# Dilated local attention plus shifted MLP on one core: 64-key attention blocks with the band mask written by TensorE, two heads per key block, source order on every engine

## The chip, the core and the metric

The kernel runs on one core of a Trainium2 chip. The metric is the device time in microseconds. Three runs of the kernel before took 226.71, 226.94 and 227.81 us; their median, 226.94 us, is the time before.

## The reference, cut to what matters

```python
x = A_x                                    # [1, 2048, 512], bf16
xn = layernorm(x)
# A: 32 heads of width 16; query s sees keys s, s-2, ..., s-14 (8 keys, dilation 2)
q, k, v = heads(xn @ wqkv)
logits = where(key >= 0, q.k * 0.25, -1e9)
s = (softmax(logits) . v) @ wo
# B: layer norm again, an MLP with four shifted column groups, a second MLP
h  = gelu(layernorm(xn) @ w1)              # 512 -> 512
hs = concat(shift(h, +1, -1, +2, -2 rows, a quarter of the columns each)) @ w2
x1 = xn + hs
h2 = gelu(layernorm(x1) @ w3) @ w4         # 512 -> 1376 -> 512
return x + s * silu(x1 + h2)
```

Because the dilation is 2, even and odd rows never attend to each other. Both kernels split the 2048 rows into two parities `p` of 1024 rows, and inside a parity the 8 keys are 8 neighbours.

## The kernel before, in words

**First half.** The 2048 rows are four chunks of 512 (two per parity). For each chunk `stage_ln` takes the layer-norm statistics (VectorE) and the power for the reciprocal root (GpSimd). `stage_a1` transposes the normalised rows on TensorE (L289) and copies them to `xnT` (L291); it also makes the row factor of the second layer norm, as four small matmuls (`rrep_ps`, L298) that spread it over the partitions. `stage_a2` multiplies by `wqk` (L317, 32 matmuls of 512 columns per chunk) and by `w1` (L329, 16 matmuls). `stage_b` multiplies by `w2` (L357) and sends the second normalised rows through DRAM to be transposed by a DMA. `stage_w3` multiplies by `w3` (L392, 44 matmuls per chunk). ScalarE takes all of these out of PSUM.

**The mask.** `kT` and `qT` exist twice per parity (e = 0, 1). In copy e the 16 rows of every second head are replaced by 16 rows of a mask factor, so that a 32-row product of keys and queries gives score plus band mask of one head. The factors are built on GpSimd (`build_mask`), written to DRAM, and `fill_mask` spreads them by 16 DMAs of 128 KB per parity and side on the SyncE queue (L224).

**Attention loop.** Nine units per parity: up to 120 queries with 128 keys. Per unit, `scores` runs 2 x 16 matmuls (L461, 32 rows, four row tiles at once) into PSUM tiles s and t, and ScalarE takes four exponentials per unit (L468, 128x960). `values` makes the V rows (L440, 4 matmuls). `weighted` multiplies the exponentials with V and a column of ones (L489, 32 matmuls, four column tiles at once) into tile o, which VectorE copies to `orw` (L496). Between these the loop lays out `w4_tile` (L413, 11 matmuls per 128 rows, one PSUM bank `w`; then VectorE L420, ScalarE tanh L422, VectorE L423) and `final_tile` (L573, 4 matmuls with `wo`; VectorE L582; addition L584).

**Softmax sums.** Three units make a run. `normalise` writes the sums to DRAM (L511), reads them back on 128 partitions (L517) and moves the outputs to `oT` by 8 GpSimd DMAs (L521). `normalise_mid` inverts (L533), writes (L534) and reads the inverses spread out (L539). `normalise_end` multiplies (L545).

**Order.** A scheduler places most instructions. In the loop the instructions wrapped in `pin` keep their source order. The loop's work is laid out by hand in the lists `fill[n]`, and the SyncE queue issues DMAs strictly one after another.

Of the kernel before, what the change touches and what calls it, by code (L numbers as in the profile page):

```python
# [11 lines left out]
F32 = mybir.dt.float32  # L12


@with_exitstack
def kernel(
# [12 lines left out]


    nc = tc.nc
    P = 128
# [15 lines left out]
    NQ = 120  # L48
    PEN = 512.0


    units = [(0, P, 0, P)]
    while units[-1][0] + units[-1][1] < M:
        q0 = units[-1][0] + units[-1][1]
        nq = min(NQ, M - q0)
        units.append((q0, nq, q0 - W, nq + W))
    NU = len(units)


    runs = []  # L60
    for cuts in ((0, 3, 6, NU), (0, 3, 6, NU)):
        runs.append(
            [(a, b, units[a][0], sum(units[u][1] for u in range(a, b))) for a, b in zip(cuts[:-1], cuts[1:])]
        )
    RW = max(r[3] for rs in runs for r in rs)
# [6 lines left out]
    big = ctx.enter_context(tc.tile_pool(name="big", bufs=12))  # L72
    mid = ctx.enter_context(tc.tile_pool(name="mid", bufs=6))
    orwp = ctx.enter_context(tc.tile_pool(name="orwp", bufs=2))
    sm4 = ctx.enter_context(tc.tile_pool(name="sm4", bufs=5))
    fin = ctx.enter_context(tc.tile_pool(name="fin", bufs=3))
    dram = ctx.enter_context(tc.tile_pool(name="dram", bufs=1, space=bass.MemoryType.DRAM))

    mask_d = dram.tile([2, 16, M], BF16, name="mask_d")
    x1n_dram = dram.tile([S, D], BF16, name="x1n_dram")  # L80

# [6 lines left out]
    cnt = {"v": 0, "a": 0, "b": 0}  # L88
# [3 lines left out]
    def layout(**tags):  # L92
        if "stack" in banks:
            banks["stack"].close()
        banks["stack"] = ctx.enter_context(ExitStack())
        for tag, n in tags.items():
            pool = banks["stack"].enter_context(tc.tile_pool(name=f"ps_{tag}", bufs=1, space=bass.MemoryType.PSUM))
            banks[tag] = (pool, n)

    def pst(tag, name):  # L100
        pool, n = banks[tag]
        return pool.tile([P, n, CH], F32, name=name, tag=tag)

    def psa(name):

        cnt["a"] += 1
        return pst("xyz"[cnt["a"] % 3], name)

    def psb(name):
        cnt["b"] += 1  # L110
        return pst("wb"[cnt["b"] % 2], name)[:, 0, :]

    layout(x=2, y=2, z=2, w=1, b=1)

    def pin(ins):
        return tc.keep_in_program_order(ins)
# [4 lines left out]
    for c in range(NCH):  # L121
        p, k = c // 2, c % 2
        n = 1 if c == 0 else 2
        for t0 in range(k * TPC, (k + 1) * TPC, n):
            nc.sync.dma_start(
                out=xn[p][:, t0 : t0 + n, :],
                in_=xv[p, t0 * P : (t0 + n) * P, :].rearrange("(i q) d -> q i d", q=P),
            )
        if c == 0:
            wqk_sb = midt([P, ND, 2 * D], "wqk_sb")  # L130
            nc.sync.dma_start(out=wqk_sb[:, :, 0:D], in_=wqkv_v[:, :, 0:D])
            nc.sync.dma_start(out=wqk_sb[:, :, D : 2 * D], in_=wqkv_v[:, :, D : 2 * D])
            w1_sb = sm4.tile([P, ND, D], BF16, name="w1_sb", tag="s4")
            nc.sync.dma_start(out=w1_sb, in_=B_w1.rearrange("(dt q) n -> q dt n", q=P))
    w2_sb = sm4.tile([P, ND, D], BF16, name="w2_sb", tag="s4")
    nc.sync.dma_start(out=w2_sb, in_=B_w2.rearrange("(g q) n -> q g n", q=P))
    w3_sb = midt([P, ND, F], "w3_sb")
    nc.sync.dma_start(out=w3_sb, in_=B_w3.rearrange("(dt q) f -> q dt f", q=P))
    wv_sb = const.tile([P, ND, D], BF16, name="wv_sb")
    nc.sync.dma_start(out=wv_sb, in_=wqkv_v[:, :, 2 * D : 3 * D])  # L140
    w4_sb = midt([P, NF, D], "w4_sb")
    nc.sync.dma_start(
        out=w4_sb[:, 0 : NF - 1, :],
        in_=B_w4[0 : (NF - 1) * P, :].rearrange("(ft q) n -> q ft n", q=P),
    )
    nc.sync.dma_start(out=w4_sb[0:FL, NF - 1, :], in_=B_w4[(NF - 1) * P : F, :])
    nc.scalar.preload_act_table_set("gelu_apprx_tanh_and_others")


    ident = const.tile([P, P], BF16, name="ident")  # L150
    make_identity(nc, ident[:])
    ones_bf = const.tile([P, P], BF16, name="ones_bf")
    nc.vector.memset(ones_bf[:], 1.0)
    nhalf = const.tile([P, TPC], F32, name="nhalf")
    nc.vector.memset(nhalf[:], -0.5)

    wm = psa("warm_ps")
    for i in range(16):
        nc.tensor.matmul(
            wm[:, i % 2, :], lhsT=ones_bf[:], rhs=ones_bf.unsqueeze(1).to_broadcast([P, TPC, P]),  # L160
            start=True, stop=True,
        )

    def build_mask():  # L170
        gp = nc.gpsimd
        tab = sm4.tile([P, 3, P + 24], BF16, name="m_tab", tag="s4")

        for i, o, v in ((0, 0, -7), (0, 15, 8), (1, 1, -7), (1, 16, 7)):
            gp.iota(
                tab[:, i, o : o + 135].rearrange("p (k t) -> p k t", t=15)[:, ::2],
                pattern=[[0, 5], [1 if o < 15 else -1, 15]], base=v, channel_multiplier=0,
                allow_small_or_imprecise_dtypes=True,
            )
        gp.memset(tab[:, 1, 0:1], -8.0)  # L180
        gp.iota(
            tab[:, 2, 0:P].rearrange("p (g k) -> p g k", k=2), pattern=[[0, P // 2], [-2, 2]], base=1,
            channel_multiplier=0, allow_small_or_imprecise_dtypes=True,
        )

        nc.vector.tensor_tensor(
            out=tab[:, :, 0:P], in0=tab[:, :, 0:P], in1=ident.unsqueeze(1).to_broadcast([P, 3, P]), op=ALU.mult
        )
        g = small.tile([P, 4], F32, name="mg", tag="mg", bufs=1)
        nc.vector.tensor_reduce(out=g[:, 0:3], in_=tab[:, :, 0:P], axis=mybir.AxisListType.X, op=ALU.add)  # L190
        sg, q = g[:, 2:3], g[:, 3:4]
        one = ones_bf[:, 0:W]
        rows = []
        for w in range(2):
            m = small.tile([P, 16, W], BF16, name=f"m_rows{w}", tag=f"mr{w}", bufs=1)
            rows.append(m)
            c, d = g[:, w : w + 1], m[:, 3:11, :]
            gp.memset(m, 0.0)
            gp.memset(d, PEN if w == 0 else 0.0)
            gp.affine_select(  # L200
                out=d, in_=d, pattern=[[1, W], [-1, W]], compare_op=ALU.is_ge if w == 0 else ALU.not_equal,
                fill=-PEN if w == 0 else 1.0, base=0, channel_multiplier=0,
            )
            gp.tensor_scalar(out=d, in0=d, scalar1=sg, scalar2=None, op0=ALU.mult)
            gp.tensor_scalar(out=q, in0=c, scalar1=-1.0 if w == 0 else 1.0, scalar2=c, op0=ALU.add, op1=ALU.mult)
            if w == 0:
                gp.tensor_scalar(out=q, in0=q, scalar1=1.0, scalar2=-PEN, op0=ALU.add, op1=ALU.mult)
                gp.tensor_scalar(out=m[:, 0, :], in0=one, scalar1=q, scalar2=None, op0=ALU.mult)
                gp.tensor_scalar(out=m[:, 1, :], in0=one, scalar1=c, scalar2=2 * PEN, op0=ALU.mult, op1=ALU.mult)
                gp.memset(m[:, 2, :], -PEN)  # L210
            else:
                gp.memset(m[:, 0, :], 1.0)
                gp.tensor_scalar(out=m[:, 1, :], in0=one, scalar1=c, scalar2=None, op0=ALU.mult)
                gp.tensor_scalar(out=m[:, 2, :], in0=one, scalar1=q, scalar2=None, op0=ALU.mult)
        for w in range(2):
            nc.sync.dma_start(out=mask_d[w].rearrange("r (g l) -> g r l", l=W), in_=rows[w])

    def fill_mask(p, w):
        t = (kT[p], qT[p])[w]
        for e in range(2):  # L220
            for gr in range(4):
                r = 32 * gr + DH * (1 - e)
                pin(
                    nc.sync.dma_start(  # L224
                        out=t[e][r : r + DH, :, :], in_=mask_d[w].unsqueeze(1).to_broadcast([DH, ND, M])
                    )
                )


    NV = 2  # L230
    v_aug = []
    for i in range(NV):
        va = const.tile([P, H, 2 * DH], BF16, name=f"v_aug{i}")
        nc.vector.memset(va[:, :, DH : 2 * DH], 2.0)
        v_aug.append(va)

    xnT = [bigt([P, ND, M], f"xnT{p}") for p in range(2)]
    kT = [[bigt([P, ND, M], f"kT{p}{e}") for e in range(2)] for p in range(2)]
    qT = [[bigt([P, ND, M], f"qT{p}{e}") for e in range(2)] for p in range(2)]
    hT = [midt([P, ND, M + 2], f"hT{p}") for p in range(2)]  # L240
    for p in range(2):
        nc.vector.memset(hT[p][:, :, 0:1], 0.0)
        nc.vector.memset(hT[p][:, :, M + 1 : M + 2], 0.0)

    def rsqrt_eps(dst, var):
# [155 lines left out]
    def w4_tile(c, jj, tail=False):  # L401
# [25 lines left out]
        return half  # L427


    oT = {}  # L430
    orw = {}

    def values(p, u):
# [283 lines left out]
```

## Time and profile before

| | |
|---|---|
| median of three runs | 226.94 us (226.71 to 227.81) |
| span of the profiled execution (first to last instruction) | 222.8 us |
| what lies around the span (median less span; the page has no other total) | 4.1 us |
| TensorE busy | 205.6 us (92%) |
| VectorE, ScalarE, GpSimd busy | 130.1, 136.2, 61.9 us |
| first matmul with `wqk` | starts at 10.06 us |
| last `w3` matmul ends, first `values` starts | 109.03 us |
| last `weighted` ends | 199.2 us |

The busy time of TensorE counts matmuls whose modelled ends overlap those of the next ones. What a matmul really costs is the distance from its start to the next start, and idle time is read from the starts.

### The profile page before, as it was taken

The numbers are of one execution on the slowest core, as the hardware profiler recorded it, in microseconds if no ns is written. First come the engines' busy times: TensorE is split into PE (matmuls) and PEld (weight loads), VectorE is DVE, ScalarE is ACT, GpSimd is POOL, SyncE is SP. The second block draws the span as 40 slices with busy tenths as digits, with TensorE's granted clock in tenths as the row PEclk, the third lists the DMA queues.
The fourth block names the chain that finished last, engine by engine and source line by source line (L and its number), as shares of the span: only waits on it lengthen the run. The fifth ranks groups of instructions, "written<-read, shape, count | busy, mean of one in ns | idle before, by whom it ended". The sixth has DMA issues, their size and how long they took to land.

```text
span 222.8 us, 4851 instructions
## 1 busy us (share of the span) xinstructions
PE 205.6 (92%) x1992; PEld 95.3 (43%) x1992; DVE 130.1 (58%) x244; ACT 136.2 (61%) x158; POOL 61.9 (28%) x119
## 2 busy tenths in 40 slices
PE   8799999999999999999869999999969999999961
PEld 2335545444444444444323444444434445454420
DVE  6689964127279683000103566678457857795984
ACT  2086696956913615665457888898776978842110
POOL 1723563502002202000000007015074482947040
PEclk9999999999999999999988999999999999999998
DMA  5999100130390675799995005526650342625222
GB/s 160 371 392 388 47 0 4 4 8 0 122 161 3 171 195 154 170 118 121 119 122 60 0 3 119 157 68 159 209 125 13 101 83 70 154 51 148 67 85 94
DMA packets 32957, 25.60 MB, mean 115 GB/s; under 512 B 16152, under 2 KB 28792, under 8 KB 32936
## 3 DMA queue, kind: packets, MB, share of 16 engines
q1 hardware_dynamic: 30312, 22.16, 42.7%
q0 software_dynamic: 1536, 2.10, 4.9%
q10 hardware_dynamic: 1088, 1.05, 1.3%
q8 instruction: 15, 0.25, 0.5%
q14 instruction: 6, 0.05, 0.1%
HBM read 16.58 MB, written 4.52 MB: 95 GB/s over the span
## 4 chain that ended last, share of the span: by engine, by line
PE 67%; DMA 10%; DVE 8%; ACT 7%; POOL 2%; SPq 2%; issue 2%; DVEq 0%; ACTq 0%
PE w_ps L413 17%; PE qk_ps L317 9%; PE w_ps L392 9%; ACT prob L468 6%; PE w_ps L329 6%; PE w_ps L357 6%; PE s_ps L461 5%; PE v_ps L440 5%; PE wo_ps L573 4%; DMA qT_159<-mask_d 4%; DMA kT_155<-mask_d 4%; PE o_ps L489 3%; DVE l1s L253 2%; SPq L224 2%; DMA oT_1494<-orw 2%
## 5 line engine op out<-in xcount | busy, mean ns | idle before, releaser
L468 ACT ACTIVATE prob<-s_ps 128x960 bf16<-128x960 f32 (+2 forms) x72 | 62.7, 925 | 15.1 <-PE s_ps L461 14.1
L413 PE MATMUL w_ps<-w_sb,h3T 128*128 128x512 bf16 (+1 forms) x176 | 44.9, 390 | 0.0
L392 PE MATMUL w_ps<-x1nT,w_sb 128*128 128x512 bf16 (+1 forms) x176 | 38.3, 379 | 0.0
L397 ACT ACTIVATE h3T<-w_ps 128x1024 bf16<-128x1024 f32 x20 | 20.5, 1024 | 25.6 <-PE w_ps L392 23.3
L521 POOL DMA_DIRECT2D oT_1494<-orw x24 | 12.4, 523 | 68.2 <-DVE orw L496 68.2
L392 PEld LDWEIGHTS <-w_sb 128*128 128x128 bf16 (+1 forms) x176 | 17.6, 100 | 20.4
L413 PEld LDWEIGHTS <-h3T 128*128 128x128 bf16 (+1 forms) x176 | 15.1, 99 | 17.3 <-issue 1.0
L496 DVE CAST orw<-o_ps 128x960 bf16<-128x960 f32 (+2 forms) x18 | 19.7, 1098 | 1.3 <-PE o_ps L489 1.1
L445 DVE CAST v_aug_148<-v_ps 128x512 bf16<-128x512 f32 (+1 forms) x9 | 6.1, 682 | 23.0 <-PE v_ps L440 23.0
L317 PEld LDWEIGHTS <-wqk_sb 128*128 128x128 bf16 x128 | 12.1, 98 | 12.9
L317 PE MATMUL qk_ps<-xnT_152,wqk_sb 128*128 128x512 bf16 x64 | 15.3, 379 | 0.8 <-DVE xnT_152 L291 0.8
L420 DVE TENSOR_TENSOR xn_95<-w_ps,xn_95 128x512 bf16<-128x512 f32 x8 | 5.5, 684 | 16.5 <-PE w_ps L413 16.5
L329 PE MATMUL w_ps<-xn2T,w_sb 128*128 128x512 bf16 x64 | 14.6, 379 | 0.0
L317 PE MATMUL qk_ps<-xnT_153,wqk_sb 128*128 128x512 bf16 x64 | 14.5, 379 | 0.0
L584 POOL TENSOR_TENSOR xo_1715<-sg,xo_1715 128x512 bf16<-128x512 bf16 x8 | 10.4, 1297 | 14.5 <-DVE sg L582 13.4
L362 DVE TENSOR_TENSOR xn_95<-w_ps,xn_95 128x1024 bf16<-128x1024 f32 x4 | 4.9, 1215 | 14.4 <-PE w_ps L357 14.4
L422 ACT ACTIVATE sig<-xn_96 128x512 bf16<-128x512 bf16 x8 | 5.0, 630 | 12.6 <-DVE xn_96 L420 12.6
L521 POOL DMA_DIRECT2D oT_2418<-orw x24 | 12.1, 513 | 1.6 <-DVE orw L496 1.6
L246 POOL TENSOR_SCALAR l3r<-l3m 128x4 f32<-128x4 f32 x4 | 0.9, 232 | 36.7 <-DVE l3m L254 36.7
L440 PE MATMUL v_ps<-wv_sb,xnT_153 128*128 128x512 bf16 (+1 forms) x36 | 9.3, 380 | 2.0 <-DVE sg L582 2.0
L461 PE MATMUL s_ps<-qT_159,kT_155 32*128 32x120 bf16 (+2 forms) x144 | 7.7, 214 | 3.1 <-DMA qT_159<-mask_d 3.1
L573 PE MATMUL wo_ps<-wo_sb,oT_2418 128*128 128x512 bf16 x32 | 7.6, 379 | 2.2 <-DVE oT_2418 L545 2.2
(132 smaller groups left out, 329.3 us busy)
## 6 DMA issues: line engine op xcount, KB each, us to landing
w_sb<-in_B_w_dram SPq DMA_DIRECT2D x1, 1376.0 KB, 9.5
w_sb<-in_B_w_dram SPq DMA_DIRECT2D x1, 1280.0 KB
wqk_sb<-in_A_wqkv_dram SPq DMA_DIRECT2D x2, 512.0 KB
w_sb<-in_B_w_dram SPq DMA_DIRECT2D x2, 512.0 KB, 6.0
xn_96<-in_A_x_dram SPq DMA_DIRECT2D x4, 256.0 KB, 6.9
xo_1715<-in_A_x_dram SPq DMA_DIRECT2D x4, 256.0 KB, 5.5
xo_2325<-in_A_x_dram SPq DMA_DIRECT2D x4, 256.0 KB, 4.5
out_dram<-xo_1715 SPq DMA_DIRECT2D x4, 256.0 KB, 3.8
```

The lines of the kernel that those rows point to most:

```text
L317: nc.tensor.matmul(pt[:, b, :], lhsT=wqk_sb[:, dt, nt * P : (nt + 1) * P], rhs=xnT[p][:, dt, cs], start=(dt == 0), stop=(dt == ND - 1),)
L329: nc.tensor.matmul(pt[:, b, :], lhsT=w1_sb[:, dt, g * P : (g + 1) * P], rhs=xn2T[:, dt, :], start=(dt == 0), stop=(dt == ND - 1),)
L357: nc.tensor.matmul(pt[:, j, :], lhsT=w2_src(p, g, m0), rhs=w2_sb[:, g, :], start=(g == 0), stop=(g == ND - 1),)
L392: nc.tensor.matmul(pt[:fs, ft % 2, :], lhsT=w3_sb[:, dt, ft * P : ft * P + fs], rhs=x1nT[:, dt, :], start=(dt == 0), stop=(dt == ND - 1),)
L397: last["gelu"] = nc.scalar.activation(h3T[:, 2 * a : 2 * a + 2, :], pt, AF.Gelu_apprx_tanh)
L413: nc.tensor.matmul(pt, lhsT=h3[c][:fs, ft, jj * P : (jj + 1) * P], rhs=w4_sb[:fs, ft, :], start=(ft == 0), stop=(ft == NF - 1),)
L440: nc.tensor.matmul(vp[:nk, :], lhsT=xnT[p][:, dt, k0 : k0 + nk], rhs=wv_sb[:, dt, :], start=(dt == 0), stop=(dt == ND - 1),)
L461: nc.tensor.matmul(st[:nk, b, i * nq : (i + 1) * nq], lhsT=kT[p][e][r : r + 32, dt, k0 : k0 + nk], rhs=qT[p][e][r : r + 32, dt, q0 : q0 + ...
L468: nc.scalar.activation(prv[:nk, 2 * h : 2 * h + 2], st[:nk, :, 0 : 4 * nq], AF.Exp, scale=SCALE)
L496: nc.vector.tensor_copy(out=orw[p][:, :, :, q0 - ra : q0 - ra + nq], in_=op[:, :, 0 : 4 * nq].rearrange("p j (s q) -> p j s q", q=nq),)
L521: nc.gpsimd.dma_start(out=oT[p][DH * hh : DH * (hh + 1), :, ra : ra + rw], in_=orw[p][32 * cg : 32 * cg + DH, jj],)
L573: nc.tensor.matmul(pt[:, j, :], lhsT=oT[p][:, dt, (i + j) * P : (i + j + 1) * P], rhs=wo["sb"][:, dt, :], start=(dt == 0), stop=(dt == ND ...
```

## The change

Every engine call goes through a wrapper that keeps it in program order, so the written order is the order on each engine. The other parts:

- **First chunks in halves.** Chunks 0 and 1 are normalised, transposed and multiplied by `wqk` in halves of 256 rows (`columns`, `qk(c, h)`). Warm-up matmuls go from 16 to 11. The row factor goes through DRAM by two DMAs (`row_factor`), not through matmuls.
- **Two heads per key block.** `kT` is one copy. `qT` holds each head pair twice, with the other head's 16 rows multiplied by zero (`sel`), so 32 rows of keys serve two heads.
- **Mask by TensorE.** `build_mask` makes two small tiles `mk`, `mq` on GpSimd; in `scores` 8 matmuls of 512 columns write the mask into PSUM and the 32 score matmuls add to it.
- **64-key blocks.** 17 units: the first 64 rows of both parities together, then 8 per parity of 120 queries, as two blocks of 64 keys by 64 queries that overlap; the overlap is added on VectorE. Per unit there is one exponential of 128x2048, and `weighted` has 64 matmuls of 64 columns.
- **Sums.** Ten runs (1, 2 x 7, 1, 1 units), inverted two units and applied three units after the last of the run.
- **V copies** go from VectorE to ScalarE.

The diff, cut to its core:

```diff
+class InOrder:
+    def __getattr__(self, name):
+        f = getattr(self.engine, name)
+        def call(*args, **kwargs):
+            return self.tc.keep_in_program_order(f(*args, **kwargs))
+        return call
...
-    NQ = 120
+    KB = P // 2
+    QU = P - W
+    NU = (M - KB) // QU
+    units = [KB - W + u * QU for u in range(NU)]
+    order = [(None, 0)] + [(p, u) for p in range(2) for u in range(NU)]
+    NN = len(order)
+    runs = [(0, 0)] + [(a, a + 1) for a in range(1, NN - 2, 2)] + [(NN - 2, NN - 2), (NN - 1, NN - 1)]
...
-    for i in range(16):
+    for i in range(11):
...
+    def row_factor(c):
...
+        pool.tensor_tensor(out=rb, in0=r2, in1=nhalf, op=ALU.pow)
+        sp.dma_start(out=row_dram[c].rearrange("(j q) -> q j", q=P), in_=rb)
+        rr = fin.tile([P, CH], BF16, name="rrow", tag="f")
+        sp.dma_start(out=rr, in_=row_dram[c].unsqueeze(0).to_broadcast([P, CH]))
...
+    def columns(c, h, evict):
...
+        if evict == "both":
+            act.activation(dst[:, :, 0:P], pt[:, :, 0, :], AF.Copy)
+            dve.tensor_copy(out=dst[:, :, P:], in_=pt[:, :, 1, :])
...
+    def qk(c, h=None, between=()):
...
+                    act.activation(qT[p][:, n0 : n0 + per, e, ms], pt, AF.Identity, scale=sel[:, e : e + 1])
...
+    stats(0, 0)
+    stats(0, 1)
+    rstd(0, 0, 2)
+    stats(0, 2)
+    norm(0, 0)
+    norm(0, 1)
+    columns(0, 0, "both")
+    stats(0, 3)
+    rstd(0, 2, 4)
+    stats(1, 0)
+    norm(0, 2)
+    norm(0, 3)
+    qk(0, 0, {6: [lambda: columns(0, 1, "dve")]})
...
+    layout(s=4, o=2, w=1, b=1)
...
+    def scores(n):
...
+        for s in range(2):
+            off = 0 if p is None or s else W
+            for r in range(4):
+                rows = slice(2 * DH * r, 2 * DH * r + 2 * DH)
+                pe.matmul(
+                    t[KB * s : KB * s + KB, r, :], lhsT=mk[rows, :],
+                    rhs=mq[rows, off : off + KB].unsqueeze(1).to_broadcast([2 * DH, 2 * ND, KB]),
+                    start=True, stop=False, tile_position=(2 * DH * r, KB * s),
+                )
+        for dt in range(ND):
+            for s in range(2):
...
+                for r in range(4):
+                    rows = slice(2 * DH * r, 2 * DH * r + 2 * DH)
+                    pe.matmul(
+                        t[KB * s : KB * s + KB, r, 2 * KB * dt : 2 * KB * (dt + 1)].rearrange("p (e q) -> p e q", e=2),
+                        lhsT=kT[pp][rows, dt, k0 : k0 + KB], rhs=qT[pp][rows, dt, :, q0 : q0 + KB],
+                        start=False, stop=(dt == ND - 1), tile_position=(2 * DH * r, KB * s),
+                    )
...
+        act.activation(pr, st.pop(n).rearrange("p r (i q) -> p r i q", q=KB), AF.Exp, scale=SCALE)
...
+    def weighted(n):
...
+            for s in range(2):
+                for cg in range(4):
+                    h = 4 * jj + cg
+                    pe.matmul(
+                        op[32 * cg : 32 * cg + 32, s, g * KB : (g + 1) * KB],
+                        lhsT=va[KB * s : KB * s + KB, dt * 8 + h, :],
+                        rhs=pr[KB * s : KB * s + KB, h // 2, 2 * dt + h % 2, :],
+                        start=True, stop=True, tile_position=(KB * s, 32 * cg),
+                    )
...
+            dve.tensor_copy(out=wide(ow, c, KB, m), in_=wide(ov_, 0, CH + W, m))
+            mix = small.tile([P, 2 * ND, W], F32, name="mix", tag="mix")
+            dve.tensor_copy(out=mix, in_=ov_[:, 1, :, 0:W])
+            dve.tensor_tensor(out=ow[:, :, c + m : c + KB], in0=ov_[:, 0, :, m:KB], in1=mix, op=ALU.add)
+        if n == b:
+            sums_out(i)
...
+    w4_at = {n: n for n in range(14)}
+    final_at = {n: divmod(n - 6, 8) for n in range(6, 17)}
+    values(0)
+    for n in range(NN):
+        scores(n)
+        gate_tanh()
+        exps(n)
+        gate_mult()
+        t = w4_at.get(n)
+        if t is not None:
+            w4_part(t, 0, 3)
+        if n in final_at:
+            final(*final_at[n])
+        if t is not None:
+            w4_part(t, 3, 6)
+        if n > 0:
+            weighted(n - 1)
+        for i, (a, b) in enumerate(runs):
+            if b == n - 3:
+                sums_apply(i)
+            if b == n - 2:
+                sums_invert(i)
+        if t is not None:
+            w4_part(t, 6, NF)
+        if n + 1 < NN:
+            values(n + 1)
...
+    weighted(NN - 1)
+    layout(f=1, g=1, h=1, i=1, o=2, w=1, b=1)
+    R = len(runs)
+    w4_part(14, 0, NF)
+    final(1, 3, "f", dve)
+    store(nc.sync, 1, 2)
+    sums_apply(R - 3)
+    sums_invert(R - 2)
+    gate_tanh()
+    gate_mult()
+    w4_part(15, 0, NF, "b")
+    sums_invert(R - 1)
+    final(1, 4, "g")
+    final(1, 5, "h")
+    gate_tanh()
+    gate_mult()
+    store(nc.sync, 1, 4)
+    sums_apply(R - 2)
+    final(1, 6, "i", dve)
+    sums_apply(R - 1)
+    final(1, 7, "f", dve)
+    store(nc.scalar, 1, 6)
```

`sums_out`, `sums_invert` and `sums_apply` hold the same steps as `normalise`, `normalise_mid` and `normalise_end`; the last run's DMAs go through ScalarE's queue. `w4_part` is `w4_tile` with the gate's tanh and multiplication moved to the start of the next unit (`gate_tanh`, `gate_mult`); `final` is `final_tile`.

## The prediction, made before the changed kernel was run

> **What bounds the kernel now.** First the page: engine totals and the chain that ended last.
>
> ```profile
> PE 205.6 (92%) x1992; PEld 95.3 (43%) x1992; DVE 130.1 (58%) x244; ACT 136.2 (61%) x158; POOL 61.9 (28%) x119
> ...
> PE 67%; DMA 10%; DVE 8%; ACT 7%; POOL 2%; SPq 2%; issue 2%; DVEq 0%; ACTq 0%
> ```
>
> TensorE bounds most of the span, but a third of the chain lies elsewhere. Then the timeline, TensorE alone, for real costs (start to next start). Sixteen `w1` matmuls at 31.84 in the chain take 3.45 us: 0.2156 us per 512-column matmul. All dense ones are 744, so 160.4 us. Transposes take 0.81/12 = 0.067 us. Sixteen score matmuls take 0.34 us; 32 of `weighted` 0.53.
>
> ```profile
> 160.55 0.39 PE L489 MATMUL o_ps<-prob,v_aug_148 64*32 64x56 bf16 x32
> 160.87 1.04 PE L440 MATMUL v_ps<-wv_sb,xnT_153 128*128 128x512 bf16 x4
> ```
>
> At 56 columns 32 of them take 0.32 us. The two sizes (56 and 120 columns) fit 0.13 us per group plus a quarter of the columns at 0.42 ns each (0.2156/512): four tiles run at once, 5.9 ns per instruction at 56 columns.
>
> Then the stages by time. Work from the first `wqk` matmul (10.06) to the last `w3` (109.03) is 432 x 0.2156 = 93.1 plus 64 transposes and row-factor matmuls at 0.067 = 4.3; only 1.6 us are idle. From 109.03 to 222.8 (113.8 us) the work is 312 x 0.2156 = 67.3 plus 18 units x (0.68 + 0.53) = 21.8, so 89; 25 us are idle. Where:
>
> ```profile
> 109.99 0.23 PE L461 MATMUL s_ps<-qT_158,kT_154 32*128 32x128 bf16 x2
> ...
> 112.29 1.28 ACT L468 ACT_TABLE_LOAD   x1 [2.42 <-PE s_ps L461]
> ...
> 114.08 0.21 PE L461 MATMUL s_ps<-qT_159,kT_155 32*128 32x128 bf16 x1 [0.98 <-DMA qT_159<-mask_d]
> ```
>
> The first scores wait 4.0 us (4.35 less 0.34 of work) for the mask DMAs of `fill_mask`. By the windows the clock is then halved:
>
> ```profile
> 112.00:114.00 2.00, 0.43 (x8) 0.14 (x6) 0.00 (x0) 1.70 (x2) 0.00 (x0) 1.00 1.06 119
> 114.00:116.00 2.00, 1.92 (x11) 0.85 (x11) 0.00 (x0) 1.52 (x2) 0.00 (x0) 0.79 1.11 123
> 116.00:118.00 2.00, 2.00 (x20) 0.67 (x18) 0.00 (x0) 0.00 (x0) 0.00 (x0) 0.50 1.06 119
> ```
>
> The third last column is the granted clock. About 3.4 us at half speed cost 1.7 us more. From 153.7 to 168.2 (14.5 us) the matmuls need 10.3; the largest part is VectorE waiting for `oT`, and TensorE behind it:
>
> ```profile
> 142.86 0.73 DVE L533 RECIPROCAL rb<-dn 128x92 bf16<-128x92 bf16 x1 [1.83 <-DMA dn<-den_d_1495]
> ...
> 165.71 0.91 DVE L545 TENSOR_TENSOR oT_1494<-oT_1494,orw 128x1440 bf16<-128x1440 bf16 x1 [2.37 <-DMA oT_1494<-orw]
> 166.53 0.68 DVE L582 TENSOR_TENSOR sg<-wo_ps,xn_95 128x512 bf16<-128x512 f32 x1
> ```
>
> Up to 198 four exponentials per unit (1.83 us a pair, 62.7 us in all) hold TensorE in most units. After 199.2 the tail is 23.6 us for 76 matmuls (16.4).
>
> **Start, in halves.** VectorE gets a third `v_aug` fill (0.48) before the statistics, which so start at 3.2, not 2.90. Each tile's statistics now end before the next begins (0.66 + 0.16 + 0.03): two tiles end at 4.9. GpSimd adds 0.23 + 1.05 (L246, L247): 6.3. Normalising at 0.36 each: 7.0. The eight transposes end at 7.45, ScalarE and VectorE copy one after the other: first `wqk` matmul 8.2 against 10.06. `wqk` is there: by the page's DMA row 1.9 MB have landed by then, and the x chunk and `wqk` are 1.5. Matmuls of 256 columns stream in 0.107, still above the 0.067 that a transpose shows with its weight load, so halves cost nothing. From 8.2: 93.1 + 56 transposes x 0.067 (3.8) + waits. I put the waits at 1.9: 0.6 for chunk 2's normalisation, 0.5 for `scaled_columns(3)` behind the mask building on GpSimd and two DMAs, 0.8 for VectorE finishing statistics before the second `w2` additions. Bounds 0.4 and 4. End of `w3`: **107.0** (before 109.03). The 11 warm-up matmuls at 0.43 end at 5.75. In this trace the warm-ups change pace at 5.9, so the clock may still be half afterwards: 0 to 1.7 us more (the 3.4 us above); I take 0, the pauses after it being about 1 us.
>
> **One unit on TensorE.** Scores: 8 matmuls of 512 columns and 32 of 128. With four tiles at once (as every row here) 2048 columns, 0.85 + 0.13 = 0.98 us; with eight (four row tiles by two column halves) 0.43 + 0.13 = 0.56. Before: 0.68. No row shows both tilings at once. Each alone reaches its full number of tiles here, so I take 0.56. `weighted`: 64 of 64 columns, 0.34 (eight at once) to 0.56 (four); at the 5.9 ns row 0.38 + 0.13 = 0.51, which I take. V stays 0.86. A unit is 2.37 (`w4`) + 0.56 + 0.51 + 0.86 = 4.31, with `final` (0.86) 5.17.
>
> The Trainium skill speaks against these pieces: TensorEngine Tiling (Array Packing), section Instruction Overhead, gives each matmul about 60 cycles and says not to tile from a dimension that is already small. At 0.42 ns per cycle, 104 matmuls would take 2.6 us per unit, and the sum below would be some 26 us longer. The 56-column row (10 ns each, group cost included) contradicts that.
>
> **One unit on ScalarE and VectorE.** The exponential of 2048 columns, by the slope of 1024 (1.024) and 448 columns (0.528), 0.86 ns each: 1.9 us. With tanh 0.63 and the V copy about 0.6 ScalarE needs 3.1 us a unit; covered by 4.31. VectorE becomes the bound of the loop. After `weighted` it must do: copy of 896 columns 1.08 (slope of L496: 1.21 at 1024, 0.61 at 448), 0.13 and 0.20 for the overlap, then reciprocal or multiplication 0.5, then the `w4` addition 0.61, with 0.2 of handovers: 2.72. Only then may the next `w4` matmul start, as bank `w` is single. Before `weighted` stand 0.65 + 0.86 + 0.65 + 0.51. Period: **5.39** with `final`, 4.53 without. The reciprocal has the `w4` addition queued behind it, and TensorE behind that.
>
> **DMA chain.** From sums written to sums readable on SyncE: 2.0 to 3.9 (median 2.6; six L511 to L517 pairs), then 1.8; inverses 1.6 undisturbed (up to 4.1), then 2.3 (up to 5.2). So the reciprocal comes 4.4 us after the copy and the multiplication 3.9 after the reciprocal. The new order gives 4.53 and 4.0: just in time. I take no wait, but 1.2 for the first run, whose 16 GpSimd DMAs take 16 x 0.51 + 2.3 = 10.5 us against two periods. GpSimd's 4.1 us of issue per run and two additions of 1.3 fit in two periods. The 32 mask DMAs leave SyncE; nothing waits for them any more.
>
> **Tail.** From unit 14 on there is no `w4` in the units, so the DMA chains show. In order: `sums_apply` of run 6 at 8.5 holds `final(16)`; last copy at 14.5; run 7's inverses queue on SyncE behind run 8's sums and land at 19.0; on ScalarE's queue the last gate's tanh stands behind the last run's DMAs, 24.5; last multiplication 27.9; last addition 30.0; store and end 3.3 (219.6 to 222.8 here). **33.3** us from unit 14.
>
> **Sum.** 107.0 + first V 0.86 + unit 0 3.8 (table load and exponential 3.3 beside 3.2) + unit 1 4.3 + 4 x 4.53 + 1.2 + 8 x 5.39 + 33.3 = **211.7** against 222.8: 2.0 gained ahead of the loop, 9.1 behind it. With the 4.1 that the median lies over the span: **215.8 us**.
>
> **Rivals.**
> - *VectorE is not the bound* and the tail is a clean chain: periods 4.31 and 5.17, tail 31, no waits in the first half (105.5): 105.5 + 4.7 + 5 x 4.31 + 8 x 5.17 + 31 = 204, so 208 us. For: 58% busy. Against: the single bank `w`.
> - *Only four tiles at once*: scores 0.98, so TensorE's 5.64 and 4.78 replace the periods: 8 x 0.25 + 4 x 0.25 + 0.8 + 1 in the tail, about 5 more: 221.
> - *Slower: VectorE waits for DMAs in every run.* Place: reciprocal and multiplication, ahead of the `w4` addition. Price: the reciprocal's wait of 1.83 and the multiplication's 0.61 (both seen at 142.9 and 151.2), for each of the seven two-unit runs, 17 us: 233. It decides from 1.6 us per run on (11.1/7). For: before, a run had about one unit more at each step and still waited three times. Against: undisturbed SyncE pairs, no mask DMAs.
> - *Source order does not hold*: the program's listing shows it holding on all engines; no chance given.
>
> A change of 0.5% (1.1 us) is about what can be told from none.
>
> **Chances.** Forecast 0.45, VectorE not the bound 0.2, four tiles 0.18, slower 0.17. A third of the last would stay near 226 or under, and a few of the four-tile cases reach it: faster 0.80, same 0.05, slower 0.15. Range 207 to 228: the low end is the first rival less 1, the high end the slower rival at seven tenths of its price (12 us), which also takes in the half clock at the start and the upper bound of the first half's waits.
>
> **What would show it.** First `wqk` matmul near 8.2, `w3` ending at 107; starts of `values` to `values` 4.5 then 5.4 apart; idle of TensorE ahead of `w4` put down to VectorE; score groups under 0.6 us; the reciprocal and `oT` rows without DMA waits; 33 us from unit 14. I am wrong if the periods exceed 6, if the reciprocal shows a DMA wait in most runs, or if score groups take near 1 us.

## The result, and the profile after

The changed kernel takes **292.4 us** (median of 4 runs, 288.2 to 296.0), the kernel before 226.8 in the runs beside it: 1.283 times as long, interval 1.270 to 1.296. The ratio and its interval, here and below, compare only the faster executions of each kernel. The forecast was 215.8 with a range up to 228. The profiled execution took 290.93 us with a span of 289.1. The page's engine totals and chain, as they were read for the kernel before:

```profile
PE 206.2 (71%) x2612; PEld 104.7 (36%) x2651; DVE 123.4 (43%) x244; ACT 108.5 (38%) x109; POOL 85.1 (29%) x169
...
PEclk9797596599579669999999999899999999975965
...
PE 41%; DMA 31%; DVE 14%; POOL 8%; issue 3%; ACT 0%; SPq 0%; DVEq 0%; POOLq 0%; ACTq 0%
```

TensorE is as busy as before (206 us), but in a span 66 us longer: the work has not grown, waits have come in. A third of the chain is DMA, and the clock row falls to 0.5 again and again in the first two fifths. The chain in order of time names the DMA, and the waits of VectorE and of the SyncE queue sum it up:

```profile
12.41 13.28 DMA row_dram<-r2b
26.61 20.98 DMA row_dram<-r2b
47.60 5.73 DMA rrow<-row_dram
53.35 1.22 DVE xn2T L25
...
73.10 19.33 DMA row_dram<-r2b
92.44 6.22 DMA rrow<-row_dram
```
```profile
DVE xn2T L25 <- DMA rrow<-row_dram: 58.6, 4, 16.6
```
```profile
SPq L25 <- DMA row_dram<-r2b: 75.0, 4, 23.0
```

`row_dram<-r2b` is the row factor's write to DRAM: 1 KB, as 512 packets of 2 bytes. It takes 13 to 23 us four times over; the read that spreads it takes 4 to 6 more. VectorE stands 58.6 us in `scaled_columns` for it. In source order the next norms are queued behind that instruction (timeline, VectorE alone):

```profile
53.35 1.22 DVE L25 TENSOR_TENSOR xn2T<-xnT,rrow 128x2048 bf16<-128x2048 bf16 x1 [16.22 <-DMA rrow<-row_dram]
54.49 1.38 DVE L25 TENSOR_SCALAR xn<-xn,l1m,l1r 128x512 bf16<-128x512 bf16 x4
```

TensorE's transposes need the norms. Behind the fourth `scaled_columns` stand the `w2` additions instead, and there `wqk` waits, whose PSUM banks they free (timeline, TensorE alone):

```profile
32.17 1.03 PE L25 MATMUL tr_ps<-ident,xn 128*128 128x128 bf16 x8 [11.64 <-DVE xn L25]
...
54.95 1.03 PE L25 MATMUL tr_ps<-ident,xn 128*128 128x128 bf16 x8 [14.73 <-DVE xn L25]
...
77.87 1.03 PE L25 MATMUL tr_ps<-ident,xn 128*128 128x128 bf16 x8 [9.61 <-DVE xn L25]
...
101.17 8.03 PE L25 MATMUL qk_ps<-xnT,wqk_sb 128*128 128x512 bf16 x23 [9.51 <-DVE xn L25]
...
161.54 0.62 PE L25 MATMUL v_ps<-wv_sb,xnT 128*64 128x512 bf16 x4
```

The windows (the third last column is the granted clock) show what such a wait costs afterwards; the last row lies inside the fourth write:

```profile
41.00:47.00 6.00, 0.00 (x0) 0.00 (x0) 0.00 (x0) 0.29 (x1) 0.00 (x0) 0.85 0.00 0
47.00:54.00 7.00, 0.00 (x0) 0.00 (x0) 0.65 (x1) 0.00 (x0) 0.00 (x0) 0.50 0.58 118
54.00:57.00 3.00, 2.05 (x11) 1.28 (x12) 2.56 (x6) 0.00 (x0) 0.00 (x0) 0.50 0.70 242
...
85.00:92.40 7.40, 6.67 (x31) 2.92 (x30) 0.00 (x0) 2.55 (x3) 0.00 (x0) 1.00 0.00 0
```

In the first and the last of them the DMA share (second last column) is 0.00 too: nothing moves while the write is not yet reported as complete.

Where the time stands against the forecast, by the profiled execution (the last column is the last kernel of the experiments):

| us | predicted | after | last kernel |
|---|---|---|---|
| first V (first `values` matmul, at the end of `w3`) | 107.0 | 161.5 | 110.3 |
| from there to the scores of unit 14 | 71.4 | 82.9 | 74.3 |
| from there to the end | 33.3 | 44.7 | 34.6 |
| outside the span | 4.1 | 1.8 | 1.8 |
| sum | 215.8 | 290.9 | 221.0 |

### The profile page after: what moved, and what is told of

It is laid out like the page before. It is cut to its first block, busy times and chain, and to the rows that moved or that the text cites. A ratio compares the mean times of both kernels' runs of the same rounds, so it can differ in the third digit from the quotient of the medians.

```text
span 289.1 us, 6221 instructions
## 1 busy us (share of the span) xinstructions
PE 206.2 (71%) x2612; PEld 104.7 (36%) x2651; DVE 123.4 (43%) x244; ACT 108.5 (38%) x109; POOL 85.1 (29%) x169
## 4 chain that ended last, share of the span: by engine, by line
PE 41%; DMA 31%; DVE 14%; POOL 8%; issue 3%; ACT 0%; SPq 0%; DVEq 0%; POOLq 0%; ACTq 0%
PE w_ps L25 25%; DMA row_dram<-r2b 19%; DMA oT<-orw 5%; PE wo_ps L25 4%; DMA rrow<-row_dram 4%; DVE orw L25 4%; POOL oT L25 3%; PE v_ps L25 3%; PE qk_ps L25 3%; PE o_ps L25 3%; DVE xn L25 3%; DMA orw<-rden_d 2%; PE s_ps L25 2%; DMA rden_d<-rb 2%; DVE l1s L25 1%
## 5 line engine op out<-in xcount | busy, mean ns | idle before, releaser
L25 POOL DMA_DIRECT2D oT<-orw x88 | 44.6, 514 | 48.2 <-DVE orw L25 48.1
L25 PE MATMUL qk_ps<-xnT,wqk_sb 128*128 128x256 bf16 (+1 forms) x190 | 33.9, 341 | 10.8 <-DVE xn L25 9.5
L25 DVE TENSOR_TENSOR xn<-w_ps,xn 128x512 bf16<-128x512 f32 (+1 forms) x24 | 20.3, 851 | 38.0 <-PE w_ps L25 38.0
L25 ACT ACTIVATE h3T<-w_ps 128x1024 bf16<-128x1024 f32 (+1 forms) x24 | 22.4, 951 | 26.2 <-PE w_ps L25 26.2
L25 ACT ACTIVATE prob<-s_ps 128x2048 bf16<-128x2048 f32 x17 | 31.7, 1865 | 0.1
L25 DVE TENSOR_TENSOR xn2T<-xnT,rrow 128x2048 bf16<-128x2048 bf16 x4 | 4.9, 1226 | 58.6 <-DMA rrow<-row_dram 58.6
L25 PEld LDWEIGHTS <-wqk_sb 128*128 128x128 bf16 x192 | 20.4, 107 | 23.2 <-issue 14.4
L25 PE MATMUL wo_ps<-wo_sb,oT 128*128 128x512 bf16 x63 | 18.8, 426 | 11.8 <-DVE oT L25 6.7
L25 ACT ACTIVATE qT<-qk_ps,sel 128x1024 bf16<-128x1024 f32 x16 | 16.8, 1112 | 22.0 <-PE qk_ps L25 22.0
L25 POOL TENSOR_TENSOR xo<-sg,xo 128x512 bf16<-128x512 bf16 x13 | 15.0, 1156 | 28.7 <-DVE sg L25 28.7
L25 DVE CAST orw<-o_ps 128x896 bf16<-128x896 f32 (+1 forms) x17 | 18.7, 1098 | 9.9 <-PE o_ps L25 9.1
L25 PE MATMUL v_ps<-wv_sb,xnT 128*128 128x512 bf16 (+1 forms) x70 | 17.4, 380 | 0.9 <-DVE sg L25 0.8
```

Source lines behind the costliest of these rows:

```text
L25: return self.tc.keep_in_program_order(f(*args, **kwargs))
```

## The experiments

Theory A: the 54 us by which the first half missed the forecast (161.5 less 107.0) are the row factor's round trip through DRAM. Theory B: they are the price of source order, whatever carries the row factor.

**Row factor by TensorE again** (all else as changed; `row_spread` and `scaled_columns` of chunk 1 behind `w1(0)`, and chunk 2's behind the norms of chunk 3).

```diff
-        sp.dma_start(out=row_dram[c].rearrange("(j q) -> q j", q=P), in_=rb)
-        sp.dma_start(out=rr, in_=row_dram[c].unsqueeze(0).to_broadcast([P, CH]))
...
+        for j in range(TPC):
...
+            dve.tensor_scalar(out=dg, in0=ident[:], scalar1=r2[:, j : j + 1], scalar2=None, op0=ALU.mult)
+            pe.matmul(rp[:, j * P : (j + 1) * P], lhsT=ones_bf[:], rhs=dg, start=True, stop=True)
...
+        act.activation(rr, rp, AF.Copy)
```

> The changed kernel with one part undone: the row factor 1/rms is spread over the partitions by TensorE again (four diagonal tiles on VectorE, four matmuls with ones, one ScalarE copy), and no longer written to DRAM and read back; the spreads stand in the source behind the w1 matmuls or norm that cover them. Theory A (the first half's loss of some 54 us, last w3 group's end 161.5 instead of 107.0 us, is the round trip of the row factor through DRAM): the last w3 group ends at 107 to 112 us, no idle of TensorE over 3 us ahead of the transposes, and the time is 290.9 minus 50 to 54, 236 to 241 us. Theory B (engines in source order lose that time whatever carries the row factor): the last w3 group ends after 140 us and the time stays above 265 us. In both, the loop and the tail keep what they lost (first V to the end about 127 us).

237.8 us (1.051 of before, 1.042 to 1.061), 54.6 less than the changed kernel. The first V starts at 113.79 instead of 161.54. The longest wait left in that half is 1.4 us. A, though 2 us later than its window. By the profiles 47.8 us of the gain lie ahead of the first V and 5.9 behind it (121.7 us to the end instead of 127.6), where the source is the same and none was expected; why is not settled.

**128 packets of 8 bytes.**

```diff
-        sp.dma_start(out=row_dram[c].rearrange("(j q) -> q j", q=P), in_=rb)
+        sp.dma_start(out=row_dram[c].rearrange("(q j) -> q j", j=TPC), in_=rb)
```

> The changed kernel with the row factor written to DRAM in another order, so that each partition's four values are 8 bytes side by side: 128 packets of 8 bytes instead of 512 of 2. The row factor then reaches the columns in permuted order (that part of the computation is changed). If the price is per packet: the write is complete in about a quarter of its 13 to 21 us, 3 to 6 us, the last w3 group ends near 115 to 125 us and the time is 245 to 255 us. If it is the place in the source order, or the queue shared with the big weight loads: 13 to 21 us a write as now, and 285 to 295 us.

251.9 us (one run); first V at 123.0. By the chain two of the writes take 4.4 and 3.6 us (by the SyncE queue the other two take 4.0 and 6.5):

```profile
22.82 4.40 DMA row_dram<-r2b
27.24 4.95 DMA rrow<-row_dram
...
53.30 3.62 DMA row_dram<-r2b
56.94 4.31 DMA rrow<-row_dram
```

**512 packets, 64 bytes apart.**

```diff
-    row_dram = dram.tile([NCH, CH], BF16, name="row_dram")
+    row_dram = dram.tile([NCH, CH * 32], BF16, name="row_dram")
...
+    for c in range(NCH):
+        sp.dma_start(out=row_dram[c].rearrange("(q s) -> q s", q=P), in_=ones_bf)
...
-        sp.dma_start(out=row_dram[c].rearrange("(j q) -> q j", q=P), in_=rb)
+        sp.dma_start(out=row_dram[c].rearrange("(j q s) -> q j s", q=P, s=32)[:, :, 0], in_=rb)
...
-        sp.dma_start(out=rr, in_=row_dram[c].unsqueeze(0).to_broadcast([P, CH]))
+        sp.dma_start(out=rr, in_=row_dram[c, 0:CH].unsqueeze(0).to_broadcast([P, CH]))
```

> The changed kernel with the 512 two-byte packets of each row factor kept, but each put 64 bytes from the next in DRAM; the read that spreads the row takes a contiguous stretch of it (so the row factor's values are not the ones computed). If the many small writes into the same stretches of DRAM are what delays the completion: it comes in 2 to 4 us and the time is 240 to 250 us. If the number of packets, or the source order, is the price: 13 to 21 us as now, 285 to 295 us.

249.1 us (one run), first V at 120.54, with the same number of packets as the changed kernel, and the same place in the order:

```profile
22.57 2.01 DMA row_dram<-r2b
24.61 4.93 DMA rrow<-row_dram
...
50.38 2.00 DMA row_dram<-r2b
52.39 5.10 DMA rrow<-row_dram
```

So the number of packets is not the price: neighbouring 2-byte values are. By the first V this kernel is still 6.8 us behind the one without the DMAs (113.79). That is the round trip itself, still some 7 us each time and in source order ahead of the norms, together with the places of two `scaled_columns`, which only the kernel without the DMAs moves; the two are not separated.

**The kernel before, with these two DMAs** in place of its matmuls.

> The kernel before, with its scheduler and everything else, but the row factor sent through the same two DMAs (512 two-byte writes to DRAM and one broadcast read) in place of its matmuls. Theory A: each of the four round trips lasts 18 to 27 us there too; as the scheduler can put other chunks' work ahead of the waiting instruction only in part, 20 to 60 us more, 247 to 287 us. Theory B (the order is the fault): within 5 us of the 226.8 of the kernel before.

256.9 us (one run), 30 more than before; the first V starts at 136.23 instead of 109.03:

```profile
19.20 18.93 DMA row_dram<-r2b
38.16 20.13 DMA xn2T<-row_dram
```

The second line is a read; it lands at 58.3, after another of the writes was issued behind it, and why it takes 20 us was not tried. Ahead of the first V the scheduler, free to put other work ahead, still loses 27 us; source order loses 48. Theory B fails as the cause, but source order does make the same wait dearer.

**The write by itself.** Nine writes of 1 KB behind the last store, each waiting for the one before.

```diff
...
+    for s in (1, 2, 4, 8, 16, 32, 64):
+        sp.dma_start(out=gap[0, 0 : CH * s].rearrange("(j q s) -> q j s", q=P, s=s)[:, :, 0], in_=src)
+    sp.dma_start(out=gap[0, 0:CH].rearrange("(q j) -> q j", j=TPC), in_=src)
+    sp.dma_start(out=gap[0, 0:CH].rearrange("(j q) -> q j", q=P), in_=src)
```

> The kernel with the row factor spread by TensorE, and behind its last store nine writes of 512 two-byte values from SBUF to one DRAM buffer, each waiting for the one before: the values 2, 4, 8, 16, 32, 64 and 128 bytes apart, then 128 packets of 8 bytes, then the order of the changed kernel (neighbouring partitions side by side). If writes into the same 64 bytes wait for each other: the first six fall from over 10 us towards 2 us as fewer share a stretch, 64 and 128 bytes apart are alike at 2 to 3 us, and 8-byte packets lie between. If it is the number of packets: all 512-packet writes take the same time. If it was the load on the queues by the weights' transfers: all take 2 to 3 us here, as nothing else moves.

Timeline of the SyncE queue (start, duration of the issue); a write's time is the distance to the next start:

```profile
234.26 0.36 SPq L25 DMA_DIRECT2D gap_dram<-gap_s  x1
248.67 0.36 SPq L25 DMA_DIRECT2D gap_dram<-gap_s  x1
257.42 0.36 SPq L25 DMA_DIRECT2D gap_dram<-gap_s  x1
261.62 0.36 SPq L25 DMA_DIRECT2D gap_dram<-gap_s  x1
264.34 0.36 SPq L25 DMA_DIRECT2D gap_dram<-gap_s  x1
266.19 0.36 SPq L25 DMA_DIRECT2D gap_dram<-gap_s  x1
267.96 0.36 SPq L25 DMA_DIRECT2D gap_dram<-gap_s  x1
269.86 0.33 SPq L25 DMA_DIRECT2D gap_dram<-gap_s  x1
272.74 0.36 SPq L25 DMA_DIRECT2D gap_dram<-gap_s  x1
```

512 values 2, 4, 8, 16, 32, 64 and 128 bytes apart: 14.4, 8.8, 4.2, 2.7, 1.9, 1.8 and 1.9 us. 128 packets of 8 bytes: 2.9. The first and the last write are the same one, the changed kernel's own order: the last took 12.4 by the waits, where the first took 14.0 and began beside the kernel's last store (nothing else moves from 237 us on). From 32 bytes apart on nothing is gained, so the stretch that neighbours share is 32 bytes, not the 64 that the expectation named. An estimate from these times: each further value in the same 32 bytes adds 0.7 to 1.0 us (14.4 less 1.9 for 15 more, 8.8 less 1.9 for 7, 4.2 less 1.9 for 3). In the changed kernel the second and third write (21.0 and 23.5 us) were issued right behind the loads of `w2` and `w3`, but the fourth (19.3 us) had no load beside it; what takes it beyond the 12.4 is not shown.

The Trainium skill, DMA: Bandwidth & Descriptors, section Specifications, says that transfers under 512 bytes are carried out as read-modify-write. That fits neighbours waiting for each other, but does not tell which of them do: 2-byte writes 32 bytes apart, under 512 bytes too, cost 1.9 us, no more than those 128 bytes apart.

**Runs applied later** (on top of the row factor by TensorE, as is all that follows).

```diff
     for n in range(NN):
+        for i, (_, b) in enumerate(runs):
+            if b == n - 4:
+                sums_apply(i)
         scores(n)
...
-            if b == n - 3:
-                sums_apply(i)
```

> On top of the kernel with the row factor spread by TensorE (237.8 us): sums_apply of a run at the start of the unit two after its inverses' DMAs are started (where VectorE waits for the gate's tanh anyway) instead of at the end of the unit after them, right ahead of the w4 addition that TensorE waits for. Theory C (each odd unit waits 0.5 to 2.1 us for the run's own DMAs, put on TensorE through the w4 addition): the waits of TensorE for that addition in units 4 to 12, 2.1 + 1.0 + 0.5 + 0.75 + 0.6 = 4.9, and 1.4 + 1.0 in units 14 and 15 go, every unit with a final is 5.6 us, and the time falls by 5 to 7 us to 231 to 233. Rival D (VectorE's own chain of instructions, not the DMAs, makes odd units longer): the odd units stay over 6 us and the time within 1.5 us of 237.8.

232.0 us (228.8 to 232.7), 5.8 less (1.014 of before, 1.005 to 1.023); by the profiles 4.4 of it lie between the first V and unit 14. The period, from one unit's scores to the next, is 4.72 without `final` and 5.58 with it. C holds. What sets those periods is seen in one unit of TensorE:

```profile
153.20 1.03 PE L25 MATMUL v_ps<-wv_sb,xnT 128*128 128x512 bf16 x4
154.16 0.42 PE L25 MATMUL s_ps<-mq,mk 32*64 32x512 bf16 x8
154.40 0.48 PE L25 MATMUL s_ps<-qT,kT 32*64 32x128 bf16 x32
154.81 0.82 PE L25 MATMUL w_ps<-w_sb,h3T 128*128 128x512 bf16 x3
155.47 1.03 PE L25 MATMUL wo_ps<-wo_sb,oT 128*128 128x512 bf16 x4
156.34 0.81 PE L25 MATMUL w_ps<-w_sb,h3T 128*128 128x512 bf16 x3
157.07 0.68 PE L25 MATMUL o_ps<-prob,v_aug 64*32 64x64 bf16 x64
157.69 1.25 PE L25 MATMUL w_ps<-w_sb,h3T 128*128 128x512 bf16 x5
158.78 0.38 PE L25 MATMUL v_ps<-wv_sb,xnT 128*128 128x512 bf16 x1
```

No row has an idle time. TensorE is the bound of the loop, though VectorE comes close (below).

**The first half, two tries.** First 17 warm-up matmuls and chunk 2's spread ahead of chunk 3's norms, on top of the first tail order below; then, on top of the second, 14 warm-ups, with the mask building moved as well:

```diff
...
+    row_factor(3)
     build_mask()
     qk(2)
-    row_factor(3)
+    row_spread(2)
...
```

> The one with the other tail, with 17 warm-up matmuls instead of 11, and the spread of the third chunk's row factor ahead of the fourth chunk's norms in the source. If the half clock after the short warm-up costs the first wqk matmuls 1.4 us and the late diagonal tiles 1.3 us: 1.5 to 3 us less, the first V group at 111 us instead of 113.8. If the matmuls only wait elsewhere afterwards: within 0.7 us.

231.1 us, no change (231.0 for the tail order it stands on): first V at 114.83. The first `wqk` matmul has the full clock, but starts at 9.34 instead of 8.42, and the chain now ends the fourth row factor behind 10 us of mask building on GpSimd.

> The one before it, with 14 warm-up matmuls, the third chunk's row spread ahead of the fourth chunk's norms, and the mask building on GpSimd behind the fourth row factor, not ahead of it (in the kernel with 17 warm-ups the chain runs 10 us through the mask building, and ends in an idle of 1.8 us ahead of the fourth spread's matmuls). If those three bound the first half: the first V group at 109 to 111 us instead of 114, 3 to 4 us less than the one without. If the chain only moves to the norms on VectorE: less than 1 us.

227.2 us (1.006 of before, 1.003 to 1.009), 3.2 less than the second tail order by itself: first V at 110.67.

**The tail, five orders.** Each moves waiting work behind ready work; the first two have the first half as it was with runs applied later, the others that with 14 warm-ups.

```diff
-    final_at = {n: divmod(n - 6, 8) for n in range(6, 17)}
+    final_at = {n: divmod(n - 6, 8) for n in range(6, 16)}
...
```

> The one with later applications, and a tail in another order: the third output tile of the second stream after the loop instead of in unit 16, where it waited 4.2 us for the DMAs of run 6; the last run's spread inverses into a buffer of their own, half of its eight transfers on SP's queue; the inverses of run 8 right behind the first w4 group after the loop; the gates' tanh ahead of the last DMAs on ScalarE's queue. If the tail's loss is TensorE standing behind DMAs that other work in the source could cover (4.2 + 1.7 + 1.8 + 3.7 + 1.6 us of idle and some 7 us at half the clock after them): 8 to 14 us less than the one with later applications, 218 to 224. If the last run's own chain of DMAs sets the end whatever the order: within 3 us of it.

231.0 us, not told apart from the 232.0 without it. `sums_apply` of run 6, in source ahead of the copies of `weighted(15)`, waits instead:

```profile
201.46 0.66 DVE L25 TENSOR_TENSOR oT<-oT,orw 128x960 bf16<-128x960 bf16 x1 [4.14 <-DMA oT<-orw]
```

```diff
+    w4_at[16] = 14
-            if b == n - 4:
+            if b == n - 4 and i < R - 4:
...
     weighted(NN - 1)
+    sums_apply(R - 4)
...
```

> The one with later applications, with the tail mended where the first attempt stopped: run 6's inverses are applied only after the last weighted's copies (before, that application stood ahead of them on VectorE and waited 4.1 us), runs 7 to 9 have their own buffers for the spread inverses, and the w4 group of tile 14 stands in unit 16, beside its exponential. If the tail's loss is work standing in the source behind DMAs it does not need: the 5.4 us of TensorE ahead of the last weighted go, the end comes at 217 to 221 us instead of 229.9, and the time is 219 to 223. If the chain sums, reciprocal, spread, multiply, projection of the last two runs sets the end: the idle moves to the last two projections and the time stays at 227 to 231.

230.4 us, again not told apart. Now the reciprocal of run 7 stands ahead of the last copies; here by the trace of the kernel with 14 warm-ups, which has the same tail:

```profile
201.01 0.53 DVE L25 RECIPROCAL rb<-dn 128x60 bf16<-128x60 bf16 x1 [4.29 <-DMA dn<-den_d]
```

```diff
-            if b == n - 2:
+            if b == n - 2 and i < R - 3:
...
     gate_mult()
+    sums_invert(R - 3)
     w4_part(15, 0, NF)
...
```

> The one with 14 warm-ups, and the tail's order mended where it stopped: there VectorE stood 4.3 us in the reciprocal of run 7, ahead of the last weighted's copies, because SP's queue held run 7's sums behind run 6's spread, which waited for the transfers out of its buffer. Now that reciprocal stands behind the last copies, run 6's spread inverses have a buffer of their own, and all eight transfers of the last run are GpSimd's again. If the order is what is left: the 6.0 us of TensorE ahead of the last w4 group go and the end moves from 225.4 to 217 to 221 us, a time of 219 to 223, below the 226 of the kernel before. If the DMA chains of the last three runs set the end (each of their DMAs took 3.5 us there instead of 1.7, beside 16 transfers in a row from GpSimd): the wait moves to the last four projections and at most 2 us are won.

228.8 us, 1.6 more than with 14 warm-ups. The reciprocal of run 9 now stands behind run 7's application:

```profile
211.68 0.66 DVE L25 TENSOR_TENSOR oT<-oT,rr 128x960 bf16<-128x960 bf16 x1 [4.15 <-DMA rr<-rden_d]
...
215.39 0.33 DVE L25 RECIPROCAL rb<-dn 128x30 bf16<-128x30 bf16 x1
```

```diff
+    def queue(i):
+        return nc.scalar if i >= R - 2 else nc.sync
...
+    inverse_write(R - 2)
+    final(1, 3, pt=last[:, 1, :])
+    inverse_write(R - 1)
+    inverse_spread(R - 2)
+    inverse_spread(R - 1)
...
```

> The one before it, with the small DMAs of the last runs no longer behind each other's waits: runs 8 and 9 have theirs on ScalarE's queue, each queue issues all that is ready before it waits (sums of both runs written, then read; both inverses written, then spread), run 7's sums are written ahead of run 6's spread, the reciprocals stand ahead of the applications that wait, and the last w4 group and four projections use banks that are free before the last copies. If the head of a queue waiting with ready work behind it is what the tail loses: recip of run 9 at 205 us instead of 215, the end at 215 to 220 instead of 227.1, a time of 217 to 222, 2 to 4 per cent below the kernel before. If each small DMA's own 3.5 us beside GpSimd's 24 transfers sets the end (four of them in a row for the last run, 14 us after the last copy, then 6 us of projection, gate and store): the end at 221 to 224, a time of 222.5 to 225.5.

227.4 us. That reciprocal comes at 205.00, as hoped, but run 8's application at 215.91, behind two projections of which the second waits for the first one's gating.

```diff
...
-    sums_apply(R - 3)
-    final(1, 4, add=dve, pt=last[:, 2, :])
-    final(1, 5, add=dve, pt=last[:, 3, :])
...
+    sums_apply(R - 3)
+    final(1, 4, "f", dve)
+    sums_apply(R - 2)
+    final(1, 5, "g", dve)
...
+    sums_apply(R - 1)
+    final(1, 6, "h", dve)
...
-    sums_apply(R - 2)
-    final(1, 6, "b", dve)
...
-    sums_apply(R - 1)
-    final(1, 7, "w", dve)
+    final(1, 7, "i", dve)
```

> The one before it, with the last two runs' applications on VectorE ahead of the gating of the projections that do not need them, and each of the last four projections in a bank of its own (in the one before, the projections of tiles 4 and 5 shared a tile and waited for each other, and the application of run 8, whose DMAs were done at some 212 us, came at 215.9). If that order is what holds the end after the last spreads: the last projection starts at 215 to 216 us instead of 219.9, the end is at 221 to 223 instead of 225.9, a time of 223 to 224.5. If the spreads themselves land only at 215 or later: no change within 1 us.

**221.5 us**, 0.981 of before (0.974 to 0.987), 5.9 less and better than the expectation's 223 to 224.5. The last four projections now run through but for a wait of 0.5 us; the last starts at 214.73 instead of 219.88.

```diff
+    keep = pst("o", "warm_ps")
+    for i in range(20):
+        pe.matmul(
+            keep[:, i % 2, :], lhsT=ones_bf[:], rhs=ones_bf.unsqueeze(1).to_broadcast([P, TPC, P]),
+            start=True, stop=True,
+        )
```

> The same with 20 matmuls of ones that nobody reads in the 5.4 us in which TensorE waits for run 7's inverses. If the half clock after that wait costs what the rows show (four projections of 1.9 us instead of 1.0, of which three in a row on the path): the end 2 to 3.5 us earlier than with the order alone, a time of 220 to 222. If the path at the end is the DMAs and VectorE: within 0.7 us of it.

220.9 us, 0.979 of before (0.970 to 0.988): not told apart from the one before it. The clock does stay up (0.90 from 201 us on; in the one before it 1.00 up to 205, then 0.69 and 0.67), but the path is not TensorE's: the projections still start only at 208.82 (209.15 before), when run 7's multiplication is done.

```profile
206.73 2.03 DVE L25 TENSOR_TENSOR oT<-oT,rr 128x960 bf16<-128x960 bf16 x1 [2.23 <-DMA rr<-rden_d]
```

## Why the prediction was wrong

**First half: the step that failed.** The prediction put the waits at 1.9 us, of which "0.5 for `scaled_columns(3)` behind the mask building on GpSimd and two DMAs", bounds 0.4 and 4. It gave the two DMAs no cost of their own, and for the same two DMAs ahead of `scaled_columns(0)` to `(2)` it put nothing and gave no reason. Measured: TensorE stood 11.6, 14.7 and 9.6 us behind the first three and 9.5 behind the fourth, 45.5 us in all. Of the 153.1 us from the first `wqk` (8.4) to the end of `w3` (161.5) some 11 are left after these and the 96.9 of work. An estimate from the granted clock in the 4 us after each wait (0.65, 0.52, 0.50, 0.50) puts 7 of them on the lower clock; and the half clock at the start, which the prediction took as 0 of up to 1.7, cost 1.3 (the first 24 `wqk` matmuls took 3.89 us, 2.57 at its 0.107 each). The nearest rows, the writes of sums and inverses at 1.6 to 4.1 us, could not show what 512 values of 2 bytes cost; that they are 2 bytes each stands in the diff, in the pattern `(j q) -> q j`. In the kernel before these two DMAs alone make 256.9 us.

**The rivals missed it too.** The slower rival sought the DMA waits in the loop; they were there (TensorE waited 2.67, 0.35, 0.66, 2.02 and 2.32 us for `w4` additions behind them), at the multiplication and not at the reciprocal, but cost 5.8 us by the experiment, a third of its 17. "Just in time: I take no wait" was the wrong reading of two durations that were equal within 0.13 us. The first wait was 2.67 instead of 1.2, and the clock after it fell to 0.57 (timeline, TensorE alone, and windows):

```profile
184.07 1.68 PE L25 MATMUL w_ps<-w_sb,h3T 128*128 128x512 bf16 x5 [2.67 <-DVE xn L25]
```
```profile
185.00:189.00 4.00, 3.67 (x74) 1.68 (x74) 2.57 (x6) 1.45 (x1) 0.00 (x0) 0.57 0.12 21
```

**The loop's bound.** VectorE's chain after `weighted` was put at 2.72 us and takes 2.43 with the row factor by TensorE (`weighted` ends at 126.17, the `w4` addition at 128.60), 2.62 with the longer reciprocal of a two-unit run; the next `w4` matmul starts at 128.87. VectorE comes close and does not decide. TensorE's unit is 4.72 and 5.58 instead of 4.31 and 5.17: V 0.96 (0.86), scores 0.65 (0.56), `weighted` 0.62 (0.51), `w4` 2.48 (2.37), each about 0.1 more. So the periods 4.53 and 5.39 were nearly right by luck, for a wrong reason: 0.19 per unit over the 12 units that they price is 2.3 us of the 2.6 (74.0 against 71.4) that remain once the runs are applied later. The first V and units 0 and 1 add 0.8 and waits left in the loop 0.7, and the 1.2 put for the first run was not paid. The Trainium skill's rule weighed there (TensorEngine Tiling (Array Packing), Instruction Overhead, about 60 cycles a matmul), read as a cost that the matmuls of a unit pay one after another, does not fit here either: 64 matmuls of `weighted` take 0.62 us, 9.7 ns each, where 60 cycles at the prediction's 0.42 ns would be 25 ns, an estimate.

**Right:** the first `wqk` at 8.2 (8.43); eight tiles at once for the scores (0.65, nearer 0.56 than 0.98); the exponential 1.9 (1.87); no wait for the mask; the exponentials no longer hold the units.

**The tail** was put at 33.3 and took 44.7 (43.1 once the runs are applied later, 34.2 with the fifth order). The waits named there came (the third output tile 4.8 us for run 6, runs 7 to 9 one behind the other), each longer than put: in the tail orders the small DMAs took 3 to 4 us beside GpSimd's transfers where 1.6 to 2.6 were taken. Order is the larger part: the fifth order wins 5.9 us over the fourth, by order and banks alone; the clock, changed by the last run alone, wins nothing that can be told. With the row factor off DRAM and these orders the parts are 110.3, 74.3 and 34.6, within 3.3 us each of the forecast's. The 4.1 us outside the span was mis-sized: it set the median of three runs against the span of a faster execution, and each run of the changed kernel took only 1.7 to 1.8 us more than its span. How much of the tail's DMA time is contention with GpSimd's transfers was not tried.

## What to carry to other kernels

Read the innermost stride of every DMA that touches DRAM: values of a few bytes written side by side from many partitions cost here far more by how many share 32 bytes than by bytes or packets. In source order the price of a wait is everything queued behind it on that engine, so put what waits behind what is ready, on DMA queues as on engines; moving one waiting instruction mostly shows the next, until the last has gone.

## What the runs showed of the hardware

- 512 two-byte writes in one DMA: 14.4 us at 2 bytes apart (12.4 by the waits with nothing else moving), 1.9 from 32 bytes apart on.
- One TensorE wait of 2.67 us in the loop already brought the clock to 0.57 between 185 and 189 us, after its end at 184; after waits of 2.02 and 2.32 us in the same loop it stayed at 1.00.
- VectorE's multiplication of 128x960 took 0.66 us in the loop and 1.5 to 2.0 in the tails of the last two kernels; why was not tried.
